# First expert layer of a pair: two products of 256 columns become one of 512, summed behind the bank

## The chip, the core and the metric

One core of a Trainium2 chip. The metric is the device time of one execution of the kernel, in microseconds, as the median of several runs. The profiled execution has its own time and a trace of every instruction of the engines: TensorE (PE, with its weight loads as PEld), VectorE (DVE), ScalarE (ACT), GpSimd (POOL) and SyncE (SP, which issues transfers).

## The reference

Block-local attention is followed by a mixture of experts. Attention: 4 batches, 8 heads, 768 positions, head size 64; each row attends to neighbours closer than 16 positions and to 24 block summaries of the keys. The second half, cut to what matters:

```python
logits = np.einsum('bsd,de->bse', x, w_gate)          # x: 4 x 768 x 512, 8 experts
...
        e = fresh_e if s == 0 or local_gate[b, s] < 0.5 else prev_e
        h = np.maximum(x[b, s] @ w1[e], 0.0)          # 512 -> 1024
        out[b, s] = p[e] * (h @ w2[e])                # 1024 -> 512
```

Every row goes through one expert, which its own logits or the row before it choose, so rows have to be sorted by expert.

## The kernel before, in words

**Attention** runs first, head pair by head pair, and writes x to memory. Beside it, and for the last batch behind it, runs the **routing**: a gate for each tile of 128 rows (`x_tile`), then, on DVE in very small instructions, the choice of the expert, the place of each row in its expert's list, and the lists by which rows are fetched and stored (`route`, `early`, `gate_p`, `finish`). Rows of one expert fill slots of 128; two slots are a **pair**. In the measured run 12 pairs and 2 single slots are multiplied. Pairs 0 to 2 belong to experts that are known early, and are multiplied while the routing of the last batch is still going on.

**Numbers are split in two.** Matmuls take a rounded 32-bit format, so each operand is a high part and a low part: `hi` and `lo` for weights, `xT[:, k, 0]` and `xT[:, k, 1]` for rows, `hT[:, f, 0]` and `hT[:, f, 1]` for the hidden layer. A product is the sum of high by high, high by low and low by high. Weights of the next expert are split by `split`: ACT casts a chunk of 1024 columns (L985), DVE or POOL subtracts (L988, L993).

**A pair** (`pair`, L1043). First layer: for each f of 8 tiles of hidden units and each k of 4 tiles of inputs, three products of 256 columns (the pair's 256 rows) at L1054, L1055 and L1056. Two f share a PSUM bank of 512 columns; there are three such banks ("s") in rotation. Behind the second f of a bank ACT takes the Relu as the high part (L1060), and DVE subtracts it from the Relu once more for the low part (L1062). Second layer: for each half of 128 rows and each f three products of 512 columns (`mm`, L1027 to L1029), then the scaled store (`store`; ACT at L1036 in pairs 0 to 2, DVE at L1039 later) and an indirect DMA. Between the products of the second layer stand the transposes of the next pair's rows (`tx`: PE L1010, ACT L1003, DVE L1005) and the splits of weights.

**The order** is written down by the program: every engine runs its own instructions in this order. `pair` is a generator that yields after every two k of the first layer and every f of the second. After each yield `flow` advances a modelled PE time `t` by 0.65 us and lets steps of the routing follow, as long as the modelled end of DVE's queue, `q`, is no more than 1.5 us ahead. A call `self.dve(cost, ready)` books DVE time in this model. So a change of these calls moves routing steps among the products.

Lines of the routing that are spoken of below: L475, L493 and L504 on PE with L484 and L496 on ACT are the gate of a tile (transpose, product, small sum; `hs` and `l` are the two copies out of PSUM). L726 makes what PE's L730 sums, L881 what L885 sums; L963 and L968 make what L972 sums, the last step of all, which gives the weights of the slots from 6 on. L793 is the first step of `finish`.

Of the kernel before, what the change touches and what calls it, by code (L numbers as in the profile page):

```python
# [9 lines left out]
F32 = mybir.dt.float32  # L10
# [3 lines left out]
AF = mybir.ActivationFunctionType  # L14
ALU = mybir.AluOpType
# [4 lines left out]
P = 128  # L20
# [10 lines left out]
E, DM, DF = 8, 512, 1024  # L31
KT, FT = DM // P, DF // P
# [31 lines left out]
class Kernel:  # L64
# [978 lines left out]
    def pair(self, i, mid, w1, w2):  # L1043

        nc = self.nc
        xT, hT = self.xT, self.hT
        for f in range(0, FT, 2):
            ps = self.bank("s").rearrange("p (f t) -> p f t", f=2)
            for j in range(2):
                for k in range(KT):  # L1050
                    c0 = k * DF + P * (f + j)
                    xh, xl = [xT[:, k, part].rearrange("p h t -> p (h t)") for part in range(2)]
                    wh, wl = [w[0][:, c0:c0 + P] for w in (self.hi, self.lo)]
                    nc.tensor.matmul(out=ps[:, j], lhsT=wh, rhs=xh, start=(k == 0), stop=False)  # L1054
                    nc.tensor.matmul(out=ps[:, j], lhsT=wh, rhs=xl, start=False, stop=False)  # L1055
                    nc.tensor.matmul(out=ps[:, j], lhsT=wl, rhs=xh, start=False, stop=(k == KT - 1))  # L1056
                    if k % 2:
                        yield
            h, l = hT[:, f:f + 2, 0], hT[:, f:f + 2, 1]
            nc.scalar.activation(out=h, in_=ps, func=AF.Relu)  # L1060
            self.dve(0.6, self.t + 0.5)
            nc.vector.scalar_tensor_tensor(out=l, in0=ps, scalar=0.0, in1=h.bitcast(F32), op0=ALU.max, op1=ALU.subtract)  # L1062
        for half in range(2):
            yp = self.bank("a")
            s = slice(P * half, P * half + P)
            for f in range(FT):
                self.mm(yp, hT[:, f, 0, s], hT[:, f, 1, s], 1, f * DM, f == 0, f == FT - 1)
                yield
                j = FT * half + f
                pm = PM if i else PM0  # L1070
                if j in pm:
                    mid(pm.index(j))
                for at, w in (PW1, w1), (PW2, w2):
                    if j in at:
                        w(*(q for q in range(4) if at[q] == j))
            self.store(yp, 2 * i + half, 2 * i < EARLY)
        yield
# [305 lines left out]
```

## Time and profile before

| | |
|---|---|
| median of 3 runs | 483.06 us (482.79 to 483.92) |
| the profiled execution | 482.07 us, its span 480.2 us |
| PE busy | 440.1 us, 92% of the span, 4400 matmuls |
| DVE, ACT, POOL busy | 254.4, 215.6 and 228.0 us |
| first layer of pairs: products | 3 x 384 of 256 columns |
| first layer of pairs: evictions | 48 on ACT (597 ns each), 48 on DVE (690 ns each) |

The span begins with the first instruction of the trace; all places in time are microseconds from there. Attention takes up to about 140 us, pairs 0 to 2 stand from 142 to 231 us, the other nine and the two single slots from there to the end. A duration of a matmul in the trace runs on beyond the start of the next one, since they are pipelined; the pace is read from the starts. A row of a timeline has its start, its duration, engine, line, operation, tiles, shapes and, in brackets, how long the engine sat idle before it and what ended that.

### The profile page before, as it was taken

The page shows a single profiled execution, that of the slowest core. Times are in us where ns is not written, and L with a number is a line of the kernel's source. Part 1 is how long each engine was busy: PE and PEld are TensorE (multiplying, and loading weights), DVE is VectorE, ACT ScalarE, POOL GpSimd, SP SyncE. Part 2 cuts the span into 40 slices and gives each one's busy share as a digit, 9 for nine tenths or more (in the row PEclk, how much of TensorE's full clock was granted, in tenths as well). Part 3 has the DMA queues.
Part 4 walks back from the last instruction along what each step waited for, and adds up shares of the span by engine and source line. Part 5 has one row for each costly group of instructions (what it writes and reads, how often), then busy time and mean ns, then how long its engine had stood idle before and what let it go on. Part 6 is the DMA issues. An engine that isn't in the chain of part 4 may idle for free. (4 is left out here: it accounts for less than half of the span.)

```text
span 480.2 us, 12079 instructions
## 1 busy us (share of the span) xinstructions
PE 440.1 (92%) x4400; PEld 382.9 (80%) x4400; DVE 254.4 (53%) x602; ACT 215.6 (45%) x479; POOL 228.0 (47%) x320
## 2 busy tenths in 40 slices
PE   7699979759879999999999999999999999999990
PEld 6577767548668779798989898989789898978980
DVE  4685677686783777994122222263656226364510
ACT  4788678667645321732111111172664117276400
POOL 2796574666612230672020202066798206678920
PEclk9999999998799999999999999999999999999996
DMA  8999869988422084193110202029399502928750
GB/s 303 394 397 365 317 213 371 328 314 308 151 78 97 1 321 163 41 343 101 46 54 35 66 23 68 22 53 375 85 353 325 173 24 58 379 85 345 261 205 26
DMA packets 23623, 92.05 MB, mean 192 GB/s; under 512 B 2927, under 2 KB 3567, under 8 KB 19440
## 3 DMA queue, kind: packets, MB, share of 16 engines
q1 hardware_dynamic: 18752, 76.11, 43.2%
q0 software_dynamic: 4640, 14.68, 9.2%
q8 instruction: 41, 0.67, 0.6%
q14 instruction: 46, 0.38, 0.3%
q10 hardware_dynamic: 144, 0.20, 0.1%
HBM read 78.40 MB, written 13.11 MB: 191 GB/s over the span
## 5 line engine op out<-in xcount | busy, mean ns | idle before, releaser
L1056 PE MATMUL bs<-xT,l 128*128 128x256 f32 x384 | 108.9, 283 | 1.2 <-DVE l L988 1.2
L1054 PE MATMUL bs<-xT,h 128*128 128x256 f32 x384 | 109.9, 286 | 0.0
L1055 PE MATMUL bs<-xT,h 128*128 128x256 f32 x384 | 108.8, 283 | 0.7 <-DVE xT L1005 0.7
L999 POOL DMA_INDIRECT xg<-x_dram,gidx x32 | 37.1, 1160 | 124.1 <-POOLq L1230 53.9
L1060 ACT ACTIVATE hT<-bs 128x512 fp32r<-128x512 f32 x48 | 28.7, 597 | 121.5 <-PE bs L1056 112.2
L1062 DVE SCALAR_TENSOR_TENSOR hT<-bs,hT 128x512 fp32r<-128x512 f32 x48 | 33.1, 690 | 90.6 <-ACT hT L1060 79.7
L1027 PE MATMUL ba<-h,hT 128*128 128x512 f32 x192 | 77.8, 405 | 0.4
L993 POOL TENSOR_TENSOR l<-stg,h 128x256 fp32r<-128x256 f32 x84 | 74.5, 922 | 2.2 <-ACT h L985 1.6
L1029 PE MATMUL ba<-h,hT 128*128 128x512 f32 x192 | 75.1, 391 | 0.0
L1028 PE MATMUL ba<-l,hT 128*128 128x512 f32 x192 | 75.0, 391 | 0.0
L1056 PEld LDWEIGHTS bs<-xT,l 128*128 128x128 f32 x384 | 73.5, 191 | 1.7 <-DVE l L988 1.7
L1055 PEld LDWEIGHTS bs<-xT,h 128*128 128x128 f32 x384 | 73.5, 191 | 1.6 <-DVE xT L1005 0.9
L1054 PEld LDWEIGHTS bs<-xT,h 128*128 128x128 f32 x384 | 73.5, 191 | 0.7 <-issue 0.2
L985 ACT CAST h<-stg 128x1024 fp32r<-128x1024 f32 x56 | 57.3, 1052 | 12.4 <-PE ba L1029 10.9
L281 ACT ACTIVATE pr<-bs,nm 128x120 f32<-128x120 f32 x192 | 51.6, 367 | 17.7 <-DVE nm L277 15.4
L988 DVE TENSOR_TENSOR l<-stg,h 128x1024 fp32r<-128x1024 f32 x35 | 47.0, 1350 | 16.2 <-ACT h L985 13.1
L1040 POOL DMA_INDIRECT out_dram<-yo,sidx x26 | 27.8, 1071 | 46.4 <-DVE yo L1039 21.3
L1027 PEld LDWEIGHTS ba<-h,hT 128*128 128x128 f32 x192 | 36.1, 188 | 8.0 <-issue 0.5
L1029 PEld LDWEIGHTS ba<-h,hT 128*128 128x128 f32 x192 | 36.0, 188 | 7.9
L1028 PEld LDWEIGHTS ba<-l,hT 128*128 128x128 f32 x192 | 36.2, 189 | 6.2
L277 DVE TENSOR_REDUCE nm<-bs 128x6 f32<-128x720 f32 x32 | 28.9, 903 | 13.1 <-ACT l L496 7.9
L302 PE MATMUL ba<-vw,pt 120*64 120x65 f32 x768 | 30.3, 228 | 4.2 <-DVE l_all L506 1.8
(236 smaller groups left out, 667.1 us busy)
## 6 DMA issues: line engine op xcount, KB each, us to landing
stg<-in_w SPq DMA_DIRECT2D x32, 1024.0 KB, 5.3
vw<-in_vW SPq DMA_DIRECT2D x16, 780.0 KB, 7.2
kp<-in_kT SPq DMA_DIRECT2D x16, 384.0 KB, 5.7
q<-in_qT SPq DMA_DIRECT2D x16, 384.0 KB, 8.1
vt<-in_vT SPq DMA_DIRECT2D x16, 384.0 KB
x_dram<-xs SPq DMA_DIRECT2D x8, 768.0 KB
wst<-in_w SPq DMA_DIRECT2D x8, 512.0 KB, 6.2
xg<-x_dram,gidx POOLq DMA_INDIRECT x32, 3.6
```

Source lines behind the costliest of these rows:

```text
L281: nc.scalar.activation(out=pr[:, h, u, :], in_=sp[:, h, u, :], func=AF.Exp, bias=nm[:, h, u:u + 1], scale=1.0)
L985: self.nc.scalar.copy(out=hi, in_=src)
L988: eng.tensor_tensor(out=lo, in0=src, in1=hi.bitcast(F32), op=ALU.subtract)
L993: eng.tensor_tensor(out=lo[:, p], in0=src[:, p], in1=hi[:, p].bitcast(F32), op=ALU.subtract)
L999: self.nc.gpsimd.indirect_dma_start(out=t, out_offset=None, in_=rows, in_offset=bass.IndirectOffsetOnAxis(ap=self.gidx[:, i:i + 1], axis=0))
L1027: nc.tensor.matmul(out=ps, lhsT=ah, rhs=wh, start=first, stop=False)
L1028: nc.tensor.matmul(out=ps, lhsT=ah, rhs=wl, start=False, stop=False)
L1029: nc.tensor.matmul(out=ps, lhsT=al, rhs=wh, start=False, stop=last)
L1054: nc.tensor.matmul(out=ps[:, j], lhsT=wh, rhs=xh, start=(k == 0), stop=False)
L1055: nc.tensor.matmul(out=ps[:, j], lhsT=wh, rhs=xl, start=False, stop=False)
L1056: nc.tensor.matmul(out=ps[:, j], lhsT=wl, rhs=xh, start=False, stop=(k == KT - 1))
L1062: nc.vector.scalar_tensor_tensor(out=l, in0=ps, scalar=0.0, in1=h.bitcast(F32), op0=ALU.max, op1=ALU.subtract)
```

## The change

In the first layer of a pair each f gets a bank of its own, and its two halves hold two sums. The high weights meet high and low rows in one product of 512 columns, so that the left half holds high by high and the right half high by low; the low weights meet the high rows in a product of 256 columns that is added to the left half. Behind the bank ACT copies the right half to SBUF (`hx`, two buffers), DVE adds it to the left half in PSUM, ACT takes the Relu as the high part, DVE makes the low part. The bank is free after that. The number of yields stays the same (16 in a first layer); the booked DVE time goes from 0.6 for two f to 0.8 for one.

```diff
-        for f in range(0, FT, 2):
-            ps = self.bank("s").rearrange("p (f t) -> p f t", f=2)
-            for j in range(2):
-                for k in range(KT):
...
-                    nc.tensor.matmul(out=ps[:, j], lhsT=wh, rhs=xh, start=(k == 0), stop=False)
-                    nc.tensor.matmul(out=ps[:, j], lhsT=wh, rhs=xl, start=False, stop=False)
-                    nc.tensor.matmul(out=ps[:, j], lhsT=wl, rhs=xh, start=False, stop=(k == KT - 1))
-                    if k % 2:
-                        yield
-            h, l = hT[:, f:f + 2, 0], hT[:, f:f + 2, 1]
-            nc.scalar.activation(out=h, in_=ps, func=AF.Relu)
-            self.dve(0.6, self.t + 0.5)
-            nc.vector.scalar_tensor_tensor(out=l, in0=ps, scalar=0.0, in1=h.bitcast(F32), op0=ALU.max, op1=ALU.subtract)
+        for f in range(FT):
+
+            ps = self.bank("s")
+            o = ps[:, 0:2 * P]
+            for k in range(KT):
+                c0 = k * DF + P * f
+                wh, wl = [w[0][:, c0:c0 + P] for w in (self.hi, self.lo)]
+                nc.tensor.matmul(out=ps, lhsT=wh, rhs=xT[:, k].rearrange("p a h t -> p (a h t)"), start=(k == 0), stop=False)
+                nc.tensor.matmul(out=o, lhsT=wl, rhs=xT[:, k, 0].rearrange("p h t -> p (h t)"), start=False, stop=(k == KT - 1))
+                if k % 2:
+                    yield
+            h, l = hT[:, f, 0], hT[:, f, 1]
+            lo = self.mw2.tile([P, 2 * P], F32, name="hx", bufs=2)
+            nc.scalar.copy(out=lo, in_=ps[:, 2 * P:4 * P])
+            self.dve(0.4, self.t + 0.5)
+            nc.vector.tensor_tensor(out=o, in0=o, in1=lo, op=ALU.add)
+            nc.scalar.activation(out=h, in_=o, func=AF.Relu)
+            self.dve(0.4, self.t + 0.9)
+            nc.vector.scalar_tensor_tensor(out=l, in0=o, scalar=0.0, in1=h.bitcast(F32), op0=ALU.max, op1=ALU.subtract)
```

In the changed kernel L1054 is the product of 512 columns and L1055 that of 256, L1060 the copy, L1062 the add, L1063 the Relu and L1065 the subtraction; lines below are three further down (the branch L1230 is L1233).

**DVE in the first layer of pair 1.** Before, between one eviction and the next (`pt`, `blk`, `eq` and `bt` are steps of `finish`):

```order
L1062 SCALAR_TENSOR_TENSOR hT<-bs,hT 128x2x256
L858 TENSOR_SCALAR e_3470<-pt 128x24
L860 TENSOR_SCALAR pt<-pt 128x24
L862 TENSOR_TENSOR blk<-o_3471,lb 128x24
L864 ISA pt<-pt,lb 128x48
L866 TENSOR_TENSOR e_3470<-e_3470,pt 128x24
L868 COPY_PREDICATED blk<-e_3470,pt 128x24
L876 TENSOR_TENSOR eq_3500<-c_81,blk 128x96
L881 TENSOR_TENSOR bt_3502<-eq_3500,c_81 128x24x4 x2
L1062 SCALAR_TENSOR_TENSOR hT<-bs,hT 128x2x256
```

The same engine and layer in the changed kernel, from the end of one bank's chain to the next bank's (`sm`, `ex`, `gr` are steps of `gate_p`, `nci`, `q` of `finish`):

```order
L1065 SCALAR_TENSOR_TENSOR hT<-bs,hT 128x256
L689 RECIPROCAL sm_3336<-sm_3336 128x6
L801 TENSOR_SCALAR nci<-nci 128x8
L691 TENSOR_TENSOR ex_3324<-ex_3324,oh 128x8x6
L804 SCALAR_TENSOR_TENSOR q<-npi,nci 128x8
L695 TENSOR_REDUCE gr_3374<-ex_3324 128x6
L1062 TENSOR_TENSOR bs<-bs,hx 128x256
L1065 SCALAR_TENSOR_TENSOR hT<-bs,hT 128x256
```

Nine instructions of the routing stood between two evictions, which came once for two f; five stand between two chains, which come once for each f, and later steps of `finish` have moved behind the layer. Between L1062 and L1065 nothing stands.

**PE at the end of pair 2.** Before, in the middle of its second layer (`ba` is the second layer's bank, `bp` what L968 writes):

```order
L1027 MATMUL ba<-h_115,hT 128x512
L1230 UNCONDITIONAL_BRANCH
L1028 MATMUL ba<-l_117,hT 128x512
L1029 MATMUL ba<-h_115,hT 128x512
L972 LDWEIGHTS A
L972 MATMUL bt<-bp,A 128x108
```

In the changed kernel, behind the last product of its second half:

```order
L1027 MATMUL ba_3962<-h_115,hT 128x512
L1028 MATMUL ba_3962<-l_117,hT 128x512
L1029 MATMUL ba_3962<-h_115,hT 128x512
L1233 UNCONDITIONAL_BRANCH x4
L972 LDWEIGHTS A
L972 MATMUL bt<-bp,A 128x108
```

The 24 products of L972 have moved from the third of 16 groups of the second layer to behind the last; pair 3's first product follows them directly. On DVE the two L1005 of pair 3's rows, which stood behind the last L968, stand ahead of it.

**ACT in the first layer of pair 0.** Before (`hs` and `l` are the copies of the gate, `wst` a weight chunk):

```order
L484 COPY hs_2873<-bt 128x512
L1060 ACTIVATE hT<-bs 128x2x256
L496 COPY l_2884<-bt 128x128
L484 COPY hs_2908<-bt 128x512
L985 CAST h_115<-wst 128x1024
L496 COPY l_2926<-bt 128x128
```

The changed kernel, at the same tiles:

```order
L484 COPY hs_2871<-bt 128x512
L1060 COPY hx<-bs 128x256
L1063 ACTIVATE hT<-bs 128x256
L496 COPY l_2883<-bt 128x128
L484 COPY hs_2902<-bt 128x512
L1060 COPY hx<-bs 128x256
L1063 ACTIVATE hT<-bs 128x256
L985 CAST h_115<-wst 128x1024
L496 COPY l_2927<-bt 128x128
```

Each copy `l` now has a copy and a Relu of a bank ahead of it, where every second one had a Relu.

More of the change, by code (lines that the diff above doesn't have):

```diff
@@ L1046, in pair @@
         xT, hT = self.xT, self.hT
-        for f in range(0, FT, 2):
-            ps = self.bank("s").rearrange("p (f t) -> p f t", f=2)
-            for j in range(2):
-                for k in range(KT):
[L1051 to L1056, printed above, removed]
-                    if k % 2:
-                        yield
-            h, l = hT[:, f:f + 2, 0], hT[:, f:f + 2, 1]
-            nc.scalar.activation(out=h, in_=ps, func=AF.Relu)
-            self.dve(0.6, self.t + 0.5)
-            nc.vector.scalar_tensor_tensor(out=l, in0=ps, scalar=0.0, in1=h.bitcast(F32), op0=ALU.max, op1=ALU.subtract)
+        for f in range(FT):
[16 more added lines that the diff above has]
+            nc.vector.scalar_tensor_tensor(out=l, in0=o, scalar=0.0, in1=h.bitcast(F32), op0=ALU.max, op1=ALU.subtract)
         for half in range(2):
```

## The prediction

> **What bounds the kernel now.** I read the page's busy times first, then busy time by stretch, then the PE timeline for the pace of matmuls, the grouped lines for durations, the DVE and ACT timelines and the waits. The rows are the page's first line and three stretches (columns: length, PE, PEld, DVE, ACT and POOL busy with their counts, granted clock, DMA share, GB/s):
>
> ```profile
> PE 440.1 (92%) x4400; PEld 382.9 (80%) x4400; DVE 254.4 (53%) x602; ACT 215.6 (45%) x479; POOL 228.0 (47%) x320
> ...
> 180.00:200.00 20.00, 20.00 (x187) 18.47 (x186) 16.92 (x72) 7.97 (x12) 5.59 (x6) 1.00 0.28 111
> 200.00:220.00 20.00, 19.13 (x154) 17.25 (x153) 18.74 (x40) 7.27 (x10) 12.70 (x12) 1.00 0.70 250
> ...
> 260.00:300.00 40.00, 40.00 (x254) 36.09 (x253) 9.86 (x14) 6.53 (x11) 6.94 (x7) 1.00 0.15 47
> ```
>
> From 260 to 300 us PE is never idle and DVE works 9.86 of 40 us: late pairs are PE-bound with free helpers. From 180 to 220 us PE is full too, but DVE is busy 35.66 of 40 us, since the routing of the last batch runs there; only 4.3 us of DVE are free. These two kinds of stretch will take the change differently.
>
> The pace of matmuls, from the PE timeline (start, duration):
>
> ```profile
> 228.12 0.39 PE L1027 MATMUL ba<-h,hT 128*128 128x512 f32 x1
> ...
> 230.16 0.39 PE L1027 MATMUL ba<-h,hT 128*128 128x512 f32 x1
> ...
> 301.29 0.28 PE L1054 MATMUL bs<-xT,h 128*128 128x256 f32 x1
> ...
> 303.93 0.28 PE L1055 MATMUL bs<-xT,h 128*128 128x256 f32 x1
> ```
>
> Nine 512-column products start in 2.04 us, 0.227 each; 22 of 256 columns in 2.64 us, 0.120 each.
>
> **The matmuls.** A (f, k) step takes three products of 256 now, 0.360 us; afterwards one of 512 and one of 256, 0.347 us. 384 such steps run (384 instructions per line, 32 a pair, 12 pairs), so PE loses 5.1 us of work, 0.43 a pair. The bounds: nothing, if a 256 behind a 512 starts later than 0.120; 10 us, if the load hidden under a 512 lets the next 256 go 0.013 earlier. I take the two rows.
>
> The Trainium skill, "TensorE: Matmul & The Clock Gate", section Back-to-back issue gap, gives a warm gap of N / 2.4 + 2.5 ns. An estimate by it is 109 and 216 ns, so a step would save 2.5 ns and the kernel 1.0 us; the trace's 120 and 227 ns disagree with both figures, and its difference, 13 ns a step, decides.
>
> **The eviction of a bank.** Before: one ACT and one DVE instruction of 512 columns for two f. Now for each f a chain of four of 256 columns, ACT copy, DVE add, ACT Relu, DVE subtract. No row has 256 columns; these have the neighbours (out<-in xcount | busy, mean ns | idle before):
>
> ```profile
> L1060 ACT ACTIVATE hT<-bs 128x512 fp32r<-128x512 f32 x48 | 28.7, 597 | 121.5 <-PE bs L1056 112.2 <-issue 9.0 <-ACT h L985 0.2
> L1062 DVE SCALAR_TENSOR_TENSOR hT<-bs,hT 128x512 fp32r<-128x512 f32 x48 | 33.1, 690 | 90.6 <-ACT hT L1060 79.7 <-ACTq L1230 10.9
> L484 ACT COPY hs<-bt 128x512 f32<-128x512 f32 x6 | 3.5, 586 | 10.5 <-PE bt L475 10.5
> L985 ACT CAST h<-wst 128x1024 fp32r<-128x1024 f32 x4 | 4.2, 1054 | 0.0
> L496 ACT COPY l<-bt 128x128 f32<-128x128 f32 x6 | 1.6, 272 | 0.9 <-PE bt L493 0.9
> L1005 DVE TENSOR_TENSOR xT<-bt,xT 128x512 fp32r<-128x512 f32 x27 | 18.4, 689 | 21.7 <-ACTq L1230 17.2 <-ACT xT L1003 2.3 <-issue 2.2
> L576 DVE TENSOR_TENSOR t<-bt,cnt 128x48 f32<-128x48 f32 x2 | 0.4, 182 | 0.0
> ```
>
> A straight line between 128 and 512 columns gives ACT 0.377 us for the copy and 0.385 for the Relu; one between 48 and 512 gives DVE 0.41 for each of its two. The ends (0.27 to 0.59, 0.18 to 0.69) are far, but I keep 0.05 to either side, as both engines' rows lie on lines.
>
> ```profile
> 263.04 0.60 ACT L1060 ACTIVATE hT<-bs 128x512 fp32r<-128x512 f32 x1 [2.28 <-PE bs L1056]
> ...
> 263.67 0.69 DVE L1062 SCALAR_TENSOR_TENSOR hT<-bs,hT 128x512 fp32r<-128x512 f32 x1 [2.19 <-ACT hT L1060]
> ```
>
> A handover costs 0.03 us (263.64 to 263.67). DVE takes its instructions in order, so from the start of the add to the end of the subtract it is held 0.41 + 0.03 + 0.385 + 0.03 + 0.41 = 1.27 us, 1.19 net of the 0.08 by which neighbours overlap (next fence), against 0.60 for two f before: 2.38 instead of 0.60 per two. In a free stretch the chain fits: PE needs 4 x 0.347 = 1.39 us a bank, the chain ends about 1.9 us behind the bank's last product, and three banks leave 2.78. So pairs 3 to 11 keep their 0.43: **-3.8 us**. If that cover goes, PE runs at the chain's pace.
>
> **Pairs 1 and 2, where DVE is full.**
>
> ```profile
> 180.44 0.16 DVE L793 TENSOR_TENSOR nbi<-cnt,adj 128x8 int32<-128x8 f32 x1
> ...
> 186.42 0.68 DVE L1062 SCALAR_TENSOR_TENSOR hT<-bs,hT 128x512 fp32r<-128x512 f32 x1
> 187.02 0.17 DVE L858 TENSOR_SCALAR e<-pt 128x24 int32<-128x24 int32 x1
> ...
> 217.80 2.02 DVE L968 TENSOR_TENSOR bp<-eqp,p 128x864 bf16<-128x864 f32 x2
> ...
> 208.81 0.87 PE L885 MATMUL bt<-bt,A 128*128 128x64 bf16 x24 [0.74 <-DVE bt L881]
> ...
> 219.87 1.33 PE L972 MATMUL bt<-bp,A 128*128 128x108 bf16 x24
> ...
> 230.84 0.28 PE L1054 MATMUL bs<-xT,h 128*128 128x256 f32 x1
> ```
>
> An L1062 holds DVE 0.60 (186.42 to 187.02). From L793 to the end of the last L968 are 39.4 us: 8 evictions, 4.8; at most 4.3 idle; 30.3 of other work. Now the same list holds 16 chains, 19.0, and by the order of rows also the two xT splits that stood behind L968 (1.4) and some ten gate steps pushed behind the first chain (1.2): 51.9 us if every idle moment is filled, 56.2 if none is. So L968 ends not at 219.8 but at 232 to 237. In PE's order all of L972 stands ahead of pair 3's first product now, and PE would reach it at about 230.84 - 1.33 - 0.86 - 0.74 = 227.9. PE must wait; whether it does so for banks inside pairs 1 and 2 or before L972 is the same time. Pair 3 starts at 233.7 to 238.3, 2.9 to 7.5 us later than 230.84. I take **+6.4**, near the upper end: idle moments of DVE are waits for other engines, which the new order does not shorten.
>
> **Pair 0, where ACT is in the way.**
>
> ```profile
> 143.26 0.39 PE L1055 MATMUL bs<-xT,h 128*128 128x256 f32 x1 [0.74 <-DVE xT L1005]
> ...
> 153.03 0.39 PE L504 MATMUL bt<-c,l 128*128 128x9 f32 x2 [0.42 <-ACT l L496]
> ...
> 154.12 0.36 PE L1054 MATMUL bs<-xT,h 128*128 128x256 f32 x1
> ...
> 164.57 0.48 PE L1027 MATMUL ba<-h,hT 128*128 128x512 f32 x1
> ```
> ```profile
> PE bt L504 <- ACT l L496: 1.3, 2, 0.9
> ```
> ```profile
> 154.45 0.59 ACT L484 COPY hs<-bt 128x512 f32<-128x512 f32 x1 [1.48 <-PE bt L475]
> 154.94 0.60 ACT L1060 ACTIVATE hT<-bs 128x512 fp32r<-128x512 f32 x1
> ```
> ```profile
> 162.85 1.41 DVE L726 TENSOR_TENSOR ebt<-c,ein 128x36 bf16<-128x36 f32 x2
> ```
>
> Here the last batch's tiles go through PE (L475, L493, L504: 1.09 us a tile, 153.03 to 154.12) between the products, and each tile's L504 waits for an ACT copy, l. That copy now stands behind a copy and a Relu that waits for DVE: hs 0.59, copy 0.38, 0.47 for the add, Relu 0.39, l 0.27, less 0.2 for two overlaps (154.45 to 154.94 for 0.59) = 1.9 us, with the matmul's tail 2.1, with a weight cast (1.05) ahead 3.0; a DVE split in the way is about as much. A tile's round is then 1.09 + 2.1 = 3.2 us, or about 4.2 (three of the six), while PE's own work for it is 1.09 + 1.39 + 0.2 = 2.7. Set out tile by tile, the six L504 start near 150.4, 154.5, 157.7, 161.0, 165.2 and 167.1, and the second layer 2.2 to 3.0 us later than 164.57: **+2.6**. Then the two L726 (1.41), which stood in the first layer, stand in the second ahead of PE's L730: **+0.8** (0 to 1.2).
>
> **The two pairs behind a single tile.**
>
> ```profile
> 360.42 0.28 PE L1054 MATMUL bs<-xT,h 128*128 128x256 f32 x1
> ...
> 365.42 0.68 DVE L1062 SCALAR_TENSOR_TENSOR hT<-bs,hT 128x512 fp32r<-128x512 f32 x1
> ...
> 444.26 0.27 PE L1054 MATMUL bs<-xT,h 128*128 128x256 f32 x1
> ...
> 449.18 0.68 DVE L1062 SCALAR_TENSOR_TENSOR hT<-bs,hT 128x512 fp32r<-128x512 f32 x1
> ```
> ```profile
> PE bs L1056 <- DVE l L988: 1.2, 2, 0.7
> ```
>
> DVE splits weights until 365.42, so the first chain ends at 365.42 + 1.27 = 366.7. PE, with 0.7 for the lows, is ready for its fourth bank at 360.42 + 0.75 + 3 x 1.39 = 365.3: 1.4 us of wait, and as much at 449.18: **+2.7** (1.5 to 3).
>
> Sum: -3.8 + 6.4 + 2.6 + 0.8 + 2.7 = +8.7 us. The profiled execution took 482.07 us (span 480.2); the median of the runs is 483.06, 1.0 above. So 482.07 + 8.7 = 490.8, and for a median 491.8.
>
> **The rivals.** *The cover holds:* chains are shorter than I think or DVE's steps slip into later gaps, and only the matmul saving is left: 483.06 - 5.1 = 478. For it: late pairs, and 11 us between L968's end and pair 3 today. Against it: DVE's 35.66 of 40 us. It decides if a chain holds DVE under about 0.55 us, so that 16 fit into 4.8 + 4.3. Chance 0.10. *Gain and loss cancel*, the early stretch costing only its lower ends: 0.05. *The clock falls while PE waits.* The trace has one such place:
>
> ```profile
> 124.00:128.00 4.00, 2.60 (x44) 0.76 0.06 21
> 128.00:132.00 4.00, 4.00 (x44) 0.50 0.42 138
> 132.00:136.00 4.00, 3.96 (x66) 0.89 0.42 124
> ```
>
> After 1.4 us of idle in 4, the clock fell to 0.50; 4 x (0.24 + 0.50 + 0.11) = 3.4 us of PE time were lost. The wait ahead of L972, some 3 us of the 6.4, would do this to pair 3 and add 2 to 3.4: 494 to 495. Chance 0.25; for it speaks this row, against it that part of the wait is spread over the banks. The Trainium skill, same page, section Why this matters for your kernels, warns of idle gaps over about 3 us, after which the clock is halved; by that rule the gap here lies at its edge, and the trace's drop after less idle time agrees in kind, not in size.
>
> **The numbers.** My forecast has 0.60: 491.8 us. Its lower ends (pair 0 at +1.5 if a round overlaps better than the tile-by-tile sum has it, L730 0, pairs 1 and 2 +2.9, behind singles +1.5, -3.8) give +2.1, 485.2; its upper ends (3.0, 1.2, 7.5, 3) 494.0, and with the clock 497.5. The matmuls' two bounds alone give 488 and 495.6, inside that. The range 485 to 497.5 leaves out the 0.15 of the first two rivals. A measurement of this kernel tells 0.2%, about 1 us, from no change: faster 0.11, same 0.04, slower 0.85.
>
> **What would show it.** Right: L1054 at 0.227 and the product behind it at 0.120; PE idle before L1054 on the DVE subtract in pairs 1 and 2; L972 waiting for L968 past 230 us; L504 waiting for l over 4 us in all; a first layer of 11.1 us in late pairs (32 x 0.347) instead of 11.5. Wrong: no PE idle between 180 and 240 us, or DVE chains under 1 us, or late pairs not shorter.

## The result and the profile after

| | before | after |
|---|---|---|
| median of the runs | 483.49 us (482.79 to 484.77, 4 runs) | 503.53 us (502.92 to 504.74, 4 runs) |
| the profiled execution, its span | 482.07, 480.2 us | 502.92, 501.1 us |

The changed kernel takes 1.0408 times as long (95% interval 1.0383 to 1.0434), 20.0 us more. The forecast was 491.8 (485.0 to 497.5): slower, as foretold, but by more than twice as much, and 6.0 us above the upper end of the range. One later run of the kernel before took 2344.28 us; no ratio below counts it.

The page's first line and its four rows of the new eviction, in the kernel after:

```profile
PE 446.9 (89%) x4016; PEld 366.6 (73%) x4016; DVE 304.8 (61%) x746; ACT 257.0 (51%) x623; POOL 220.2 (44%) x320
...
L1063 ACT ACTIVATE hT<-bs 128x256 fp32r<-128x256 f32 x96 | 36.9, 385 | 59.2 <-DVE bs L1062 59.2
L1065 DVE SCALAR_TENSOR_TENSOR hT<-bs,hT 128x256 fp32r<-128x256 f32 x96 | 40.8, 425 | 43.3 <-ACT hT L1063 43.3
...
L1060 ACT COPY hx<-bs 128x256 f32<-128x256 f32 x96 | 35.7, 372 | 52.5 <-PE bs L1055 50.3
...
L1062 DVE TENSOR_TENSOR bs<-bs,hx 128x256 f32<-128x256 f32 x96 | 41.2, 429 | 21.6 <-ACT hx L1060 16.2
```

Read the means first. The copy takes 372 ns, the Relu 385, the add 429, the subtraction 425; the straight lines gave 377, 385, 410 and 410. DVE has 50.4 us more to do than before, ACT 41.4. PE has fewer products but is busy 6.8 us longer; its mean granted clock is 0.965 now and was 0.980.

Where the time went is read from the PE timeline: the first product of each layer, and the two products that waited longest.

```profile
145.45 0.50 PE L1054 MATMUL bs<-xT,h 128*128 128x512 f32 x1 [1.04 <-DVE xT L1005]
...
171.49 0.48 PE L1027 MATMUL ba<-h,hT 128*128 128x512 f32 x1
...
186.58 0.50 PE L1054 MATMUL bs<-xT,h 128*128 128x512 f32 x1
...
200.12 0.47 PE L1027 MATMUL ba<-h,hT 128*128 128x512 f32 x1
...
215.95 0.76 PE L885 MATMUL bt<-bt,A 128*128 128x8 bf16 x24 [3.15 <-DVE bt L881]
216.56 0.72 PE L1054 MATMUL bs<-xT,h 128*128 128x512 f32 x1
...
231.85 0.39 PE L1027 MATMUL ba<-h,hT 128*128 128x512 f32 x1
...
247.71 0.54 PE L972 MATMUL bt<-bp,A 128*128 128x108 bf16 x4 [3.01 <-DVE bp L968]
...
249.82 0.78 PE L1054 MATMUL bs<-xT,h 128*128 128x512 f32 x1
```

The same starts, taken from the PE timeline of every kernel that follows, give this table: when pair 0's first product that needs the low parts of its rows starts (DVE's L1005 makes them, and this ends attention here; the form before has one product of 256 columns ahead of it; the instructions ahead of pair 0's first layer are the same and in the same order in before and after), the length of each layer of pairs 0 to 2 (first layer / second layer), the time from pair 3 to the start of the last product, and the sum of all behind attention. Us throughout.

| kernel | rows ready | pair 0 | pair 1 | pair 2 | pair 3 to end | sum |
|---|---|---|---|---|---|---|
| before | 143.26 | 21.31 / 13.97 | 13.43 / 12.36 | 13.18 / 13.33 | 237.41 | 324.99 |
| after | 145.45 | 26.04 / 15.09 | 13.54 / 16.44 | 15.29 / 17.97 | 238.54 | 342.91 |
| e1_late | 145.77 | 21.33 / 13.97 | 13.43 / 12.36 | 13.17 / 13.69 | 237.32 | 325.27 |
| e2_early | 145.66 | 26.05 / 15.69 | 13.56 / 16.44 | 15.29 / 17.96 | 237.94 | 342.93 |
| e3_pairs12 | 144.01 | 21.32 / 14.14 | 12.37 / 16.95 | 15.34 / 14.52 | 238.22 | 332.86 |
| e4_pair0 | 145.83 | 25.87 / 16.54 | 13.20 / 13.15 | 13.65 / 13.13 | 237.42 | 332.96 |
| e5_old_bookings | 146.89 | 25.33 / 14.16 | 15.97 / 13.93 | 16.98 / 14.78 | 237.64 | 338.79 |
| e6_no_add | 146.50 | 21.19 / 14.13 | 13.09 / 12.39 | 13.76 / 13.04 | 236.29 | 323.89 |
| e7_three_256 | 145.90 | 26.17 / 15.31 | 13.52 / 16.45 | 15.32 / 17.97 | 239.65 | 344.39 |
| e8_skew | 145.25 | 26.31 / 17.97 | 12.43 / 18.40 | 14.03 / 19.74 | 245.70 | 354.58 |
| e9_fill | 144.78 | 26.03 / 16.00 | 13.52 / 16.44 | 15.27 / 16.99 | 237.50 | 341.75 |
| e10_late_by_twos | 143.56 | 21.32 / 13.96 | 13.43 / 12.35 | 13.17 / 13.68 | 235.80 | 323.71 |
| e11_skew_early | 143.93 | 25.96 / 14.83 | 14.10 / 13.11 | 17.67 / 13.09 | 237.79 | 336.55 |
| e12_static_late | 145.79 | 21.34 / 13.96 | 13.42 / 12.36 | 13.18 / 13.33 | 234.86 | 322.45 |

The first two lines hold the result. Behind attention the kernel is 17.9 us longer: pair 0 +5.9, pair 1 +4.2, pair 2 +6.8, everything else +1.1. Pairs 1 and 2 lose mainly in their second layers, whose products were not changed.

Which waits these are, PE's own over pairs 0 to 2, in two answers (us in total, times, longest): first 140 to 172 us, then 170 to 252.

```profile
PE bt L504 <- ACT l L496: 4.4, 4, 1.6
```
```profile
PE bt L885 <- DVE bt L881: 3.2, 1, 3.2
PE bt L972 <- DVE bp L968: 3.0, 1, 3.0
PE bs L1054 <- DVE hT L1065: 1.2, 2, 0.9
PE bt L1010 <- DMA xg<-x_dram,gidx: 0.9, 2, 0.5
```

And the clock, from stretches of the kernel after (length, PE, PEld, DVE, ACT and POOL busy with counts, granted clock, DMA share, GB/s). Before, the same part of the program ran at 1.00.

```profile
158.00:162.00 4.00, 4.00 (x29) 3.18 (x25) 1.67 (x7) 2.34 (x5) 2.04 (x3) 0.58 0.00 0
212.00:216.00 4.00, 0.85 (x6) 0.39 (x5) 3.90 (x10) 2.16 (x3) 2.08 (x3) 1.00 0.00 0
216.00:220.00 4.00, 4.00 (x35) 3.52 (x36) 3.72 (x16) 0.37 (x1) 1.92 (x2) 0.58 0.15 24
244.00:247.00 3.00, 0.69 (x4) 0.23 (x2) 2.97 (x4) 0.69 (x1) 1.30 (x1) 1.00 0.02 5
247.00:251.00 4.00, 3.29 (x28) 3.16 (x29) 0.92 (x2) 0.00 (x0) 0.56 (x1) 0.57 0.17 66
```

Two stretches in which PE stands still and DVE is full, each followed by one at half clock, and a third behind the waits of L504. 0.58 in 4 us is 4 x 0.42 / 0.5 = 3.4 us at half speed.

### The profile page after: what moved, and what is told of

It is laid out like the page before. It is cut to its first block, busy times and chain, and to the rows that moved or that the text cites. A ratio compares the mean times of both kernels' runs of the same rounds, so it can differ in the third digit from the quotient of the medians.

```text
span 501.1 us, 11658 instructions
## 1 busy us (share of the span) xinstructions
PE 446.9 (89%) x4016; PEld 366.6 (73%) x4016; DVE 304.8 (61%) x746; ACT 257.0 (51%) x623; POOL 220.2 (44%) x320
## 3 DMA queue, kind: packets, MB, share of 16 engines
HBM read 78.40 MB, written 13.11 MB: 183 GB/s over the span
## 5 line engine op out<-in xcount | busy, mean ns | idle before, releaser
L1054 PE MATMUL bs<-xT,h 128*128 128x512 f32 x384 | 141.9, 410 | 4.3 <-DVE hT L1065 3.1
L1055 PE MATMUL bs<-xT,l 128*128 128x256 f32 x384 | 109.0, 284 | 0.2
L999 POOL DMA_INDIRECT xg<-x_dram,gidx x32 | 38.7, 1209 | 127.5 <-POOLq L1233 52.5
L1054 PEld LDWEIGHTS bs<-xT,h 128*128 128x128 f32 x384 | 73.6, 192 | 24.7 <-DVE hT L1065 6.4
L1027 PE MATMUL ba<-h,hT 128*128 128x512 f32 x192 | 78.0, 406 | 0.4
L1055 PEld LDWEIGHTS bs<-xT,l 128*128 128x128 f32 x384 | 73.9, 193 | 1.2 <-DVE l L988 0.8
L993 POOL TENSOR_TENSOR l<-stg,h 128x256 fp32r<-128x256 f32 x84 | 59.7, 746 | 18.3 <-ACT h L985 18.1
L1063 ACT ACTIVATE hT<-bs 128x256 fp32r<-128x256 f32 x96 | 36.9, 385 | 59.2 <-DVE bs L1062 59.2
L1065 DVE SCALAR_TENSOR_TENSOR hT<-bs,hT 128x256 fp32r<-128x256 f32 x96 | 40.8, 425 | 43.3 <-ACT hT L1063 43.3
L985 ACT CAST h<-stg 128x1024 fp32r<-128x1024 f32 x56 | 57.2, 1053 | 11.6 <-PE ba L1029 10.7
L1060 ACT COPY hx<-bs 128x256 f32<-128x256 f32 x96 | 35.7, 372 | 52.5 <-PE bs L1055 50.3
L988 DVE TENSOR_TENSOR l<-stg,h 128x1024 fp32r<-128x1024 f32 x35 | 51.0, 1474 | 10.7 <-ACT h L985 9.2
L1062 DVE TENSOR_TENSOR bs<-bs,hx 128x256 f32<-128x256 f32 x96 | 41.2, 429 | 21.6 <-ACT hx L1060 16.2
L1040 POOL DMA_INDIRECT out_dram<-yo,sidx x26 | 32.4, 1246 | 48.8 <-DVE yo L1039 25.2
L1027 PEld LDWEIGHTS ba<-h,hT 128*128 128x128 f32 x192 | 36.1, 188 | 8.3 <-issue 1.2
```

The source lines that it names most:

```text
L985: self.nc.scalar.copy(out=hi, in_=src)
L988: eng.tensor_tensor(out=lo, in0=src, in1=hi.bitcast(F32), op=ALU.subtract)
L993: eng.tensor_tensor(out=lo[:, p], in0=src[:, p], in1=hi[:, p].bitcast(F32), op=ALU.subtract)
L999: self.nc.gpsimd.indirect_dma_start(out=t, out_offset=None, in_=rows, in_offset=bass.IndirectOffsetOnAxis(ap=self.gidx[:, i:i + 1], axis=0))
L1027: nc.tensor.matmul(out=ps, lhsT=ah, rhs=wh, start=first, stop=False)
L1054: nc.tensor.matmul(out=ps, lhsT=wh, rhs=xT[:, k].rearrange("p a h t -> p (a h t)"), start=(k == 0), stop=False)
```

## The experiments

Two theories were set against each other. **Load:** a bank holds DVE for its whole chain, some 1.2 us, and the full DVE of pairs 0 to 2 makes PE wait. **Order:** the raised bookings (0.8 us a bank instead of 0.6 for two) push the steps of the routing behind the first layers, and PE waits for L881 and L968 because they were put late. Beside them stood the clock, what the wider product is worth, and whether the loss is only early.

**Where the loss stands: e1_late, e2_early, e3_pairs12, e4_pair0.** The edit in each is a condition on the pair's number in front of the two forms of the first layer:

```python
if i >= 3:      # e1_late;  i < 3: e2_early;  i in (1, 2): e3_pairs12;  i == 0: e4_pair0
    ...         # the new form
else:
    ...         # the form before
```

> Pairs 0 to 2 as in the kernel before, the new form from pair 3 on. Taken from the two traces, the stretch from pair 3's first product to the end of the last second layer grew by 1.1 us (237.4 to 238.5 us). Theory 'all of the loss stands in pairs 0 to 2': within 1.2 us of the kernel before (482.4 to 484.7 for 483.5); by the terms of the prediction for this part (-3.8 and +2.7) 482.4. Rival 'the new form loses everywhere, since the chain of four instructions paces it': over 488 us. If the products saved what was forecast and the two places behind singles cost nothing: 479.7.

> The new form in pairs 0 to 2 alone, the form before from pair 3 on. Theory 'all of the loss stands in pairs 0 to 2': 501 to 503 us, and the first second layer of pair 3 begins some 19 us later than before. Rival 'the loss is spread over the kernel': under 495. In the trace of the changed kernel attention, whose code is the same, ended 2.2 to 3.3 us later; if that is an accident of one execution, 498 to 500 us.

> The new form in pairs 1 and 2 alone. The term of the prediction for this part was +6.4 us: 489.9. By the traces pairs 1 and 2 took 10.9 us longer: 494.4, with PE idle before L885 and before L972, about 3 us each, and a stretch of half clock behind each of the two. Rival 'pair 0 delays the routing and the later waits are only its echo': under 488 us and no wait over 1.5 us at L885 and L972.

> The new form in pair 0 alone. The terms of the prediction for this part were +2.6 and +0.8 us: 486.9. By the traces pair 0 took 4.7 us longer: 488.2. If what pair 0 loses is won back, since pairs 1 and 2 then wait less for the routing than they would: under 485. If attention, which ended 2.2 to 3.3 us later in the changed kernel, is delayed by pair 0's new form: 491.

Measured, beside a median of 483.8 us of the kernel before (17 runs on the same chip, with the long one): late alone 485.93 (ratio 1.0039, interval 1.0019 to 1.0060), early alone 504.08 (1.0414, 1.0379 to 1.0450), pairs 1 and 2 alone 492.59 (1.0189, 1.0153 to 1.0226), pair 0 alone 490.27 (1.0120, 1.0083 to 1.0158).

The early form alone brings back the whole loss, and its median lies 1.1 us above the upper end expected: 342.93 us behind attention, as the changed kernel's 342.91. The late form is worth nothing either way: 325.27 against 324.99. Its median (it too lies 1.2 us above the end expected) is 2.1 us above the kernel before; in the two profiles attention ends 2.5 us later, and 0.9 us more lie behind the start of the last product. More on attention below. The two early parts add up to less than the whole: +7.9 and +8.0 alone, +17.9 together. PE's waits in e3_pairs12, 170 to 252 us, show why:

```profile
PE bt L885 <- DVE bt L881: 2.6, 1, 2.6
PE bt L972 <- DVE bp L968: 1.3, 1, 1.3
```

L972 waits 1.3 us there, and 3.0 with pair 0 in the new form as well. So the waits are no echo of pair 0, but pair 0 makes them longer; 492.6 lies between the forecast's term and what the trace of the changed kernel would give. In the table pairs 1 and 2 take 6.9 us longer there than before, and 10.9 in the changed kernel. Pair 0 alone costs more than the 5.9 us that its layers cost in the changed kernel: 7.1 in pair 0, where a stretch of half clock (170 to 174 us) falls into the second layer, and 0.8 in pairs 1 and 2, which wait for the routing that pair 0 delays. Its 490.27 us lie 2.1 above what the traces gave, near the 491 of the case of a delayed attention; but attention ended at 145.83 us there and at 145.77 in e1_late, where pair 0 has the form before.

**Load or order: e5_old_bookings.**

```diff
-            self.dve(0.4, self.t + 0.5)
+            if f % 2:
+                self.dve(0.6, self.t + 0.5)
...
-            self.dve(0.4, self.t + 0.9)
```

> The changed kernel with DVE time booked as in the kernel before (0.6 once for two f), so that the routing's steps stand among the products where they stood. Theory 'load' (DVE is held 1.2 us a bank, whatever the order): 501 to 505 us, as the changed kernel's 503.5; the waits only change their places. Rival 'order' (the higher bookings pushed L881 and L968 behind, and the two long waits of PE come from that): the waits at L885 and L972 fall under 1 us each and the two stretches of half clock behind them go: 492 to 495.

500.32 us (ratio 1.0361, 1.0299 to 1.0423, beside 484.21; its four runs go from 499.36 to 504.93), below what load foretold, far above what order did. PE's waits, 170 to 252 us, and DVE's last step of the routing:

```profile
PE bs L1054 <- DVE hT L1065: 4.3, 4, 1.6
PE bt L885 <- DVE bt L881: 1.9, 2, 1.1
PE bt L972 <- DVE bp L968: 1.6, 1, 1.6
...
PE bt L950 <- DVE tot L944: 1.5, 1, 1.5
```
```profile
235.97 1.05 DVE L968 TENSOR_TENSOR bp<-eqp,p 128x864 bf16<-128x864 f32 x1
```

The routing ends 10.6 us earlier than in the changed kernel (237.02 against 247.65), yet pairs 1 and 2 take 61.7 us instead of 63.2: PE waits 4.3 us for banks (L1054) instead of 1.2, and still 5.0 for the routing, L944 among it, another of its steps. No wait is longer than 1.6 us, and no stretch of half clock lies behind the start of pair 0. So most of the loss stays whatever the order; the order places the waits, and the places are worth 4.1 us (338.79 against 342.91 behind attention).

**Without the chain: e6_no_add.** The copy and the add are left out, and with them the high-by-low part of the output; bookings as in e5_old_bookings.

```diff
-            lo = self.mw2.tile([P, 2 * P], F32, name="hx", bufs=2)
-            nc.scalar.copy(out=lo, in_=ps[:, 2 * P:4 * P])
-            self.dve(0.4, self.t + 0.5)
-            nc.vector.tensor_tensor(out=o, in0=o, in1=lo, op=ALU.add)
             nc.scalar.activation(out=h, in_=o, func=AF.Relu)
-            self.dve(0.4, self.t + 0.9)
+            if f % 2:
+                self.dve(0.6, self.t + 0.5)
```

> The products of the changed kernel without the copy and the add, so that the high-by-low half is left out of the output: a bank's eviction is a Relu and a subtraction of 256 columns, 0.42 us of DVE a bank, and the bookings are as before. Theory 'load': DVE holds 0.85 us for two f instead of 0.60, the early stretch is within 2 us of the kernel before and nothing waits over 1.5 us at L885 or L972: 482 to 488 us. Rival 'the loss comes from one bank for each f, not from the chain': over 494.

483.21 us beside 484.21 (ratio 0.9986, 0.9963 to 1.0009): no loss is left. The subtraction's row in the groups (count | busy, mean ns | idle before):

```profile
L1062 DVE SCALAR_TENSOR_TENSOR hT<-bs,hT 128x256 fp32r<-128x256 f32 x96 | 40.4, 423 | 80.8 <-ACT hT L1059 78.7 <-issue 2.0
```

One bank for each f, twice as many evictions, DVE held 0.42 us a bank: all that is harmless. Between this kernel and e5_old_bookings stand only the copy and the add with what waits for them, and 14.9 us (323.89 against 338.79). ACT's copy and DVE's add go together here; which of the two weighs more is not shown.

**The wider product by itself: e7_three_256.**

```diff
-                nc.tensor.matmul(out=ps, lhsT=wh, rhs=xT[:, k].rearrange("p a h t -> p (a h t)"), start=(k == 0), stop=False)
+                xh, xl = [xT[:, k, part].rearrange("p h t -> p (h t)") for part in range(2)]
+                nc.tensor.matmul(out=o, lhsT=wh, rhs=xh, start=(k == 0), stop=False)
+                nc.tensor.matmul(out=ps[:, 2 * P:4 * P], lhsT=wh, rhs=xl, start=False, stop=False)
```

> The changed kernel's banks, evictions and bookings, with three products of 256 columns in place of one of 512 and one of 256. It tells what the wider product is worth by itself. By the late pairs of the trace (11.29 us instead of 11.51) about 0.22 us a pair where PE does not wait: 505 to 506 us. By the prediction's 0.43 a pair: 507 to 508. If PE's pace counts in the early pairs as well, since every delay there lengthens the waits: over 508.

504.56 us (ratio 1.0430, 1.0400 to 1.0459), 1.0 us above the changed kernel and 0.4 below the least that was expected. In the table pairs 1 and 2 are the same to 0.03 us a layer with the slower products: PE's pace does not count there. Late first layers take 11.51 us again instead of 11.29. Pair 3 to the end is 1.1 us longer, not the 2.0 of nine such layers, mainly since the second layer ahead of the second single slot takes 12.28 us instead of 13.35.

**DVE not standing still: e8_skew, e11_skew_early.** Between its add and its subtraction DVE waits for the Relu, 7.2 us over the 16 banks of pairs 1 and 2. Here the subtraction of a bank goes behind the next bank's add; e8_skew does so in all pairs with the raised bookings, e11_skew_early in pairs 0 to 2 with the bookings of the kernel before.

```diff
-            self.dve(0.4, self.t + 0.9)
-            nc.vector.scalar_tensor_tensor(out=l, in0=o, scalar=0.0, in1=h.bitcast(F32), op0=ALU.max, op1=ALU.subtract)
+            if kept is not None:
+                low()       # the subtraction for the bank before
+            kept = (o, h, l)
+        low()
```

> The changed kernel with each bank's subtraction moved behind the next bank's add on DVE, so that DVE does not stand still for the Relu between the two: by the trace's rows a bank then holds DVE some 0.75 us instead of 1.22, 7.5 us less over the 16 banks of pairs 1 and 2. Theory 'load': the waits at L885 and L972 fall from 6.2 us together to under 1.5 and the stretches of half clock behind them go: 491 to 496 us. Rival 'order' (the bookings stay as they are): 501 to 504, as the changed kernel. If banks come free too late, PE waits before L1054 in every pair: over 504.

> The changed kernel with the bookings of the kernel before, and in pairs 0 to 2 each bank's subtraction behind the next bank's add on DVE. Beside the kernel with these bookings alone (500.3 us) it takes only the standing still of DVE for the Relu out of the chain, some 0.45 us a bank. Theory 'load' (how long a bank holds DVE sets the early stretch): pairs 1 and 2 take 4 to 7 us less, 493 to 496 us. Rival 'a bank that is free later costs as much': 499 to 502. If it is worse for the early pairs too, as the skew in all pairs was with the raised bookings: over 503.

e8_skew: 513.28 us (ratio 1.0590, 1.0552 to 1.0627), in the third case, but only the late pairs got there by a wait for banks. PE's waits in it, 170 to 256 us:

```profile
PE bt L972 <- DVE bp L968: 4.8, 1, 4.8
PE bt L885 <- DVE bt L881: 4.6, 1, 4.6
```

The first layers of pairs 1 and 2 became 1.1 and 1.3 us shorter, but the routing ended no sooner: DVE's steps from L793 to the last L968 take 59.0 us, in the changed kernel 58.7, under the same raised bookings. So PE waited longer at L885 and L972. Pair 0's second layer took 17.97 us instead of 15.09, with a wait of 1.8 us at L1010 for the gather of pair 1's rows. Beside that, late first layers took 11.94 us instead of 11.29: a bank comes free only after the next one's add. In pair 4 the subtraction of the first bank ends at 283.98 us, and the fourth bank's first product starts at 284.13, 0.27 us behind the product ahead of it instead of 0.12.

e11_skew_early: 496.48 us (ratio 1.0257, 1.0231 to 1.0283). Its waits, 170 to 252 us:

```profile
PE bs L1061 <- ACT hT L1071: 2.4, 3, 1.9
PE bt L885 <- DVE bt L881: 0.8, 1, 0.8
```

With the standing still taken out and the steps of the routing let in, pairs 1 and 2 take 58.0 us instead of 61.7, 3.7 us less and so just short of the 4 to 7 expected; the median lies 0.5 above its range. Taken together, from the table, pairs 0 to 2 take 104.4 us in the changed kernel, 101.2 with the old bookings, 108.9 with the skew, 98.8 with both, and 87.6 before and in e6_no_add. So the skew gained 2.4 us with the old bookings and lost 4.5 with the raised ones: taking load off DVE helped only in the order that let the routing use it.

**The clock: e9_fill.**

```diff
+            if s0 == EARLY:
+                for _ in range(FILL):        # FILL = 40; the same loop stands ahead of L972
+                    nc.tensor.matmul(out=m[:, 0:P], lhsT=self.wz, rhs=self.wz, start=True, stop=True)
             for t in range(NT):
                 nc.tensor.matmul(out=m[:, 0:2 * n], ...)      # L885
```

> The changed kernel with 40 idle products (128 columns of zeros, overwritten by what follows) put ahead of L885 and as many ahead of L972 on PE, which cost nothing while PE would have waited there 3.1 and 3.0 us. Theory 'a wait of PE brings a stretch of half clock behind it': the two stretches behind these waits go, 1.7 us each, and the kernel takes 499.5 to 501 us instead of 503.5. Rival 'the stretches fall where they do for other reasons': 503 to 504, or more if the products are in the way.

500.58 us (ratio 1.0353, 1.0320 to 1.0386; the changed kernel's interval begins at 1.0383, so the two touch). The same stretches as of the changed kernel above:

```profile
212.00:216.00 4.00, 3.26 (x45) 2.80 (x44) 3.90 (x9) 2.38 (x3) 2.30 (x4) 1.00 0.00 0
216.00:220.00 4.00, 3.83 (x42) 3.42 (x42) 3.72 (x17) 0.37 (x1) 1.70 (x2) 1.00 0.13 16
244.00:247.00 3.00, 3.00 (x44) 2.67 (x43) 2.96 (x4) 0.69 (x1) 0.70 (x1) 1.00 0.06 18
247.00:251.00 4.00, 3.22 (x37) 2.90 (x35) 1.10 (x2) 0.24 (x1) 0.74 (x1) 1.00 0.19 70
```

PE still waits 0.9 us at L885 and 0.8 at L972, instead of 3.2 and 3.0, and the clock stays at 1.00: the long waits do bring the stretches. But the price of 1.7 us each was wrong for the first one. Pair 2's first layer takes 15.27 us with the full clock and 15.29 with the half, since there DVE is late next:

```profile
PE bs L1060 <- DVE hT L1071: 2.7, 2, 2.5
```

PE ran ahead and waited 2.5 us for a bank instead of 0.9. Only the second stretch, behind which PE has no more waits, was worth its 1.4 us (pair 2's second layer 16.99 instead of 17.97, pair 3's first layer 11.18 instead of 11.62). Behind attention the profile has 1.2 us of the 3 by which the medians differ.

**A better order of products: e10_late_by_twos, and the version that beats both: e12_static_late.** e10 is e1_late with two products of 512 columns and then two of 256 in every group; e12 has that form in pairs 3 to 7 alone.

```diff
+            for k0 in range(0, KT, 2):
+                for k in (k0, k0 + 1):
+                    wh = self.hi[0][:, k * DF + P * f:k * DF + P * f + P]
+                    nc.tensor.matmul(out=ps, lhsT=wh, ...)
+                for k in (k0, k0 + 1):
+                    wl = self.lo[0][:, k * DF + P * f:k * DF + P * f + P]
+                    nc.tensor.matmul(out=o, lhsT=wl, ...)
+                yield
```

> As the kernel with the new form from pair 3 on alone (485.9 us; a step of the first layer at 0.353 us, the 512-column product taking 0.235 behind one of 256), but two products of 512 columns and then two of 256. Theory 'a product of 512 pays for standing behind one of 256': one of two goes at 0.227, a step at 0.349, a late first layer falls from 11.29 to 11.16 us, and the kernel gains 1.0 us: 484.9. Rival 'the pace is of the mixture, not of the order': 11.29 and 485.9. If the weights of two short products in a row are late: over 486.5.

> The new form with two products of 512 and then two of 256 in pairs 3 to 7 alone: these follow no single slot, while the later ones can, and there the new form cost more than it gave (12.74 and 12.72 us for a first layer behind a single slot instead of 12.50 and 12.42, and 25.25 instead of 24.60 for the second single slot with the layer before it). Theory: five first layers of 11.14 us instead of 11.51 give 1.85 us, 0.35 are lost at the end of pair 2, nothing behind the single slots: 1.5 us below the kernel before, 483.0 where that stands at 484.5. Rival 'the second layers and the code give it back': within 0.5 us of the kernel before.

The pace in the changed kernel and in e10_late_by_twos, in late pairs:

```profile
273.97 0.40 PE L1054 MATMUL bs<-xT,h 128*128 128x512 f32 x1
274.21 0.28 PE L1055 MATMUL bs<-xT,l 128*128 128x256 f32 x1
274.33 0.40 PE L1054 MATMUL bs<-xT,h 128*128 128x512 f32 x1
```
```profile
277.41 0.62 PE L1055 MATMUL bs<-xT,h 128*128 128x512 f32 x2
277.86 0.40 PE L1058 MATMUL bs<-xT,l 128*128 128x256 f32 x2
278.10 0.63 PE L1055 MATMUL bs<-xT,h 128*128 128x512 f32 x2
```

Alternating, a step takes 0.353 us (11.29 us for 32), the next product starting 0.24 us behind a wide one here and 0.12 behind a narrow one. By twos, two wide ones take 0.45 and two narrow ones 0.24, a late first layer 11.14 us, 0.348 a step: what the separate rows of 0.227 and 0.120 had promised. But alternation alone does not cost the 0.005 us a step. In pair 3 of e9_fill, at full clock, it has the faster pace:

```profile
249.46 0.40 PE L1060 MATMUL bs<-xT,h 128*128 128x512 f32 x1
...
259.86 0.39 PE L1060 MATMUL bs<-xT,h 128*128 128x512 f32 x1
```

These are 30 steps in 10.40 us, 0.347 each, and pair 3 of the changed kernel has the same 0.347 behind its half clock (254.50 to 259.70 us, 15 steps). What sets the one pace or the other was not tried; by twos every late layer had the faster one.

e10: 483.58 us beside 484.52 (ratio 0.9991, 0.9973 to 1.0008), 1.3 us below the kernel before behind attention. e12: 480.58 beside 484.23 (ratio 0.9935, 0.9905 to 0.9964), 2.5 us below it behind attention, where 1.5 was expected: the five layers give 1.9, nothing is lost at the end of pair 2 (13.33 us in both), and 0.7 more stand in the layer behind the first single slot (11.81 us instead of 12.50); why was not tried. That is 0.65% faster than the kernel before; what the medians have above the 2.5 us lies outside that stretch. It keeps the form before wherever a single slot may come first, and in pairs 0 to 2.

## Why the prediction was right or wrong

**Direction and mechanism: right; the size: wrong by 9.2 us behind attention (17.9 instead of 8.7), of which pairs 1 and 2 are 4.5.** The chain holds DVE, DVE is full beside pairs 0 to 2, and PE waits for l at L504 (4.4 us in all, over 4 as foretold) and for L968 past 230 us. e6_no_add settles it by taking the chain's copy and add away.

**The matmuls, -3.8: half the size.** The step "I take the two rows", 0.227 and 0.120, put together paces that had been read in runs of equal products. In most late pairs a step takes 0.353 us, not 0.347; pair 3 of e9_fill, with 0.347, shows that the sum was possible, but it was not the rule. A pair keeps 0.22 us (11.29 instead of 11.51), nine pairs 2.0, which leaves 1.8 of the miss. The rival order in e10_late_by_twos has 0.37 a pair.

**Pairs 1 and 2, +6.4 (2.9 to 7.5): 10.9; this step failed most.** For these pairs alone the term was nearly right: in e3_pairs12 they take 6.9 us longer, and DVE's list from L793 to the end of the last L968 takes 56.2 us (181.20 to 237.44), the upper end that was worked out. What failed is the sum, which adds the terms of pair 0 and of pairs 1 and 2 as if, beyond 1.2 us of gate steps, neither touched the other. With pair 0 in the new form as well the list is longer. These are DVE from L793 to the end of the last L968 in the kernel after, before, and DVE's largest wait in it after:

```profile
189.00:247.65 58.65, 51.01 (x316) 40.36 (x314) 46.28 (x147) 23.78 (x50) 19.21 (x21) 0.97 0.38 147
```
```profile
180.40:219.80 39.40, 38.60 (x333) 35.19 (x332) 35.06 (x111) 15.24 (x21) 18.29 (x17) 1.00 0.49 179
```
```profile
DVE hT L1065 <- ACT hT L1063: 7.2, 16, 0.5
```

The list takes 58.7 us, 2.4 more than alone. DVE is idle 12.4 us in it; 7.2 of these lie inside the chains, where the prediction had counted them, and the other 5.2 stand against its "at most 4.3". PE's wait ahead of L972 grows from 1.3 us in e3_pairs12 to 3.0, and now a stretch of half clock follows it, worth 1.0 us of pair 2 by e9_fill. That is 3.4 of the 4.0 us between 6.9 and 10.9; the rest was not taken apart.

The sentence that it is the same time whether PE waits for banks or before L972 failed too, by less. In e5_old_bookings, with waits of 1.6 us at most, pairs 1 and 2 take 1.5 us less than bunched into 3.2 and 3.0 us ahead of L885 and L972. The prediction shows L885's row but sets no wait there.

**The clock, a rival with 0.25 and one place: it came in three.** At L504, L885 and L972. Its size, 2 to 3.4 us a place, was too high: 1.4 us behind L972 and none behind L885 by e9_fill, some 0.7 in pair 0's first layer (26.04 with the stretch, 25.33 without it in e5_old_bookings, whose bookings differ). The trace of before had two such places, not one: its clock is 0.50 from 109 to 112 us as well.

**Pair 0, +2.6 and +0.8: 4.7 and 1.1.** From the start of the layer, the six L504 were set at 7.1, 11.2, 14.4, 17.7, 21.9 and 23.8 us. The four in the kernel after that waited:

```profile
152.99 0.39 PE L504 MATMUL bt<-c,l 128*128 128x9 f32 x2 [0.62 <-ACT l L496]
157.32 0.39 PE L504 MATMUL bt<-c,l 128*128 128x9 f32 x2 [1.60 <-ACT l L496]
...
164.84 0.39 PE L504 MATMUL bt<-c,l 128*128 128x9 f32 x2 [0.64 <-ACT l L496]
169.16 0.39 PE L504 MATMUL bt<-c,l 128*128 128x9 f32 x2 [1.58 <-ACT l L496]
```

The first, second, fourth and fifth start 7.5, 11.9, 19.4 and 23.7 us behind 145.45: the right waits, but the rounds were longer than worked out, and the half clock came from 158.6 us on. PE waited 4.4 us here where it had waited 1.3. The other term came by another way. L730 waits for nothing, but the lists that it leads to are late, the gather of pair 1's rows with them, and L1010 waits 0.9 us for the DMA.

**Behind a single slot, +2.7: 1.0.** The wait at L1054 is there (0.9 us each). But the layers behind a single slot were already 1.0 and 0.9 us longer than others before (12.50 and 12.42 instead of 11.51), and that was counted as new. They are now 0.27 longer each (12.77 and 12.69), which with the 0.22 that the products give back makes 0.5 each.

**What was not in the sum.** The second single slot, with the layer before it, took 26.25 us instead of 24.60: there L1027 waits 1.4 us for an ACT cast (L985), on an engine that now has two instructions a bank. Pair 3's first layer begins at half clock and has 0.3 us more than the other late ones. With these the terms as measured come to about 17.7 of the 17.9 us. And attention, whose code is the same, ended 2.2 us later in the profile (145.45 against 143.26). Over the 14 profiles it ends between 143.26 and 146.89, in kernels with the new form and without; the kernel before was profiled in the earliest of them, so the 1.0 us from its profile to its median was too little. About 2 us of the 20.0 of the medians lie outside the 17.9 behind attention; whether a kernel's form shifts its attention is left open.

## What to carry to other kernels

An edit that gives TensorE a few nanoseconds and pays on VectorE has to be judged where VectorE is full: here the form cost 17.9 us where it stood in pairs 0 to 2 alone (e2_early), and with its products by twos it won in pairs 3 to 7 (e12_static_late), so it is worth a condition on the stage. Terms of stages that share a full engine do not simply add: +7.9 and +8.0 alone were +17.9 together. On an in-order engine count how long a chain holds it, standing still included, not its busy time; and when a booked cost changes an order, ask which wait it bunches. Read a pace in the mixture that will run, and in several layers, not from runs of equal instructions.

## What the runs showed of the hardware

- A wait of TensorE is followed by a stretch of half clock, 3.4 us long in the kernel after, if the wait is long enough. Waits of 3.0 us and more (L885 and L972 after, in e2_early and in e7_three_256) always had one; 2.6 us had one (e3_pairs12), 2.5 had none (e9_fill), and the waits of 1.6 at L504 had one or not in the same code. Row by row, 1 us each, in the kernel after:

```profile
158.00:159.00 1.00, 1.00 (x10) 0.90 (x7) 0.00 (x0) 0.26 (x1) 1.00 (x2) 0.80 0.00 0
159.00:160.00 1.00, 1.00 (x8) 0.69 (x7) 0.37 (x1) 0.60 (x2) 1.00 (x2) 0.50 0.00 0
...
162.00:163.00 1.00, 1.00 (x15) 0.82 (x8) 0.84 (x1) 0.12 (x1) 0.00 (x0) 0.99 0.00 0
...
247.00:248.00 1.00, 0.29 (x4) 0.30 (x5) 0.65 (x1) 0.00 (x0) 0.56 (x1) 0.68 0.00 0
```

  (0.20 + 3 x 0.50 + 0.01) / 0.5 = 3.4 us for the first stretch. The Trainium skill, "TensorE: Matmul & The Clock Gate", section What's actually happening, has the clock set in windows of 3413 ns that run freely, without regard to the program. The length agrees, and the rows show where the windows begin: the stretches start where the clock leaves 1.00, at 158.60 us (0.80 in its row), 216.64 (0.82 from 216 to 217) and 247.36 (0.68), which is 17 and 9 times 3.413 us apart. When every trace is laid out in windows on its own grid, what counts behind attention is how long PE is idle inside one window. Idle is the window's length less PE's busy time in it. All 9 full-clock windows with 1.9 us of idle or more are followed by half clock, none of the 1330 with under 1.4 us is, and the 17 with 1.45 to 1.77 us came out both ways (9 at half, 8 at full). So the wait of 2.5 us in e9_fill, with 1.6 us in one window and 0.9 in the next, had none. A place in the window does not explain all: 1.60 us inside one window halved the clock in the kernel after (155.19 to 158.60) and not in e5_old_bookings (155.49 to 158.91).
- Products of zeros count for the clock: with 40 of them in 2.4 us ahead of L972 it stayed at 1.00 (e9_fill), without them it fell to 0.50.
- The half clock cost nothing where TensorE would only have reached its next wait sooner (pair 2's first layer, 15.27 and 15.29 us).
